# Two spectral-plus-MLP layers on one core: filter reversal in runs of four bins, merged mirror-class multiplies, rows of x issued from two queues

## The chip, the cores and the metric

The kernel runs on one core of one Trainium2 chip. The metric is the device time of one execution in microseconds (us). Most executions of a kernel here agree within 0.3%, which is some 3 us (the four of the kernel before lie within 2.7 us), and medians of four to six runs still leave about 1 us open; for smaller differences the document uses stage times from the profiles, one profiled execution of each kernel. In the profile of the kernel before, TensorE multiplies (6063 multiplies), VectorE and ScalarE work element by element and empty PSUM (775 and 504 instructions), POOL (GpSimd) and SP mostly issue DMA transfers (96 of POOL's 102 instructions).

## The reference, cut to what matters

```python
def _A_ref(x, w_r, w_i):                       # spectral layer
    X = rfft2(x.astype(float32)) * (w_r + 1j * w_i)
    return irfft2(X, s=(S, D)).astype(bfloat16)
def _B_ref(x, w1, b1, w2):                     # MLP
    h = x @ w1 + b1
    return (h * tanh(softplus(h))) @ w2

x = x + _A_ref(_layernorm(x), ...); x = x + _B_ref(_layernorm(x), ...)
x = x + _A_ref(_layernorm(x), ...); x = x + _B_ref(_layernorm(x), ...)
```

x is 2048 x 1024, the MLP is 3584 wide, everything is bf16 at the borders. Both layers of a kind share their weights.

## The kernel before

The Fourier transforms are factored into multiplies by constant tables. The first spectral layer goes: load x; row statistics on VectorE and ScalarE; a first transform (`s1`), which needs the rows of x in another order (XR) and tables scaled by each row's 1/deviation; then eight software-pipelined steps, each with the second transform (`s2`), the filter's preparation (`filter_bins`), the third transform and filter product (`s3`), and the way back (`i1`, `i2`); at last the back transform of the rows (`i4`).

Loading, and what runs beside it:

```python
    def prologue(self):
        for c in range(4):
            self.dma(sp, self.XS[:, 4*c:4*c+4, :], xt[...], f"x{c}", writes=...)
        # ... M0, IDF, JT from SP
        for q in range(4):
            for h in range(8):
                self.dma(sp, self.XR.ap[h:P:8, 32*q:32*q+32, :], xv[h][...], f"xr{q}", parts=[r])
        self.dma(sp, self.FD[:], self.con["FD"], "fd", writes=[self.r_fd])
        self.op(self.pool, lambda e: e.memset(self.EPS[:], 1e-5), writes=[self.r_eps, self.r_warm])
        self.warm(ACT.Sqrt)          # ScalarE: an activation that reads EPS, to load its table (1.28 us in the profile)
```

`first_scales` lets VectorE do the statistics of 10 tiles of x and ScalarE those of 6 (behind `warm` in ScalarE's queue), then one square root over all rows. The evacuations and the filter's reversal:

```python
    # s1: PSUM to Y
    if j % 2: ...activation...           # ScalarE
    else:     ...tensor_copy...          # VectorE
    # i2: PSUM to U; VectorE if the condition holds, else ScalarE
    if (g > 4 and (g < 7 or half == 0)) or (half == 0 and g % 2 and li): ...
    # filter_bins: a multiply by a reversed identity mirrors the bins, one multiply for each residue of 8
    for kd in (1, 2, 3):
        mov = wr.ap[:, c, src, :].rearrange("p (i k) -> p k i", k=8)[:, 7 - kd, :]     # every 8th bin
        fns.append(... e.matmul(ps[:, col:col + 64], jt[:, j:j + P], mov, ...))
```

## Time and profile before

| | before |
|---|---|
| median of the runs beside the changed kernel | 1054.78 us (1053.77 to 1056.46, 4 runs) |
| profiled span | 1051.8 us |
| first transform starts (first of its multiplies) | 25.25 us |
| eight steps start | 46.33 us |
| back transform of the first layer starts | 127.11 us |
| second layer: first transform, steps, back transform start | 550.72, 562.30, 633.67 us |

The three starts of the first layer are the rulers of this document. They are read off the timeline as the first multiply of each stage. "Steps" below means the time from the second start to the third, 80.78 us here; it contains the DMA round trip before the back transform, for which TensorE waits 11.95 us here, and which no part of the change touches.

### The profile page before, as it was taken

The numbers are of one execution on the slowest core, as the hardware profiler recorded it, in microseconds if no ns is written. First come the engines' busy times: TensorE is split into PE (matmuls) and PEld (weight loads), VectorE is DVE, ScalarE is ACT, GpSimd is POOL, SyncE is SP. The second block draws the span as 40 slices with busy tenths as digits, with TensorE's granted clock in tenths as the row PEclk, the third lists the DMA queues.
The fourth block names the chain that finished last, engine by engine and source line by source line (L and its number), as shares of the span: only waits on it lengthen the run. The fifth ranks groups of instructions, "written<-read, shape, count | busy, mean of one in ns | idle before, by whom it ended". The sixth has DMA issues, their size and how long they took to land. (4 is left out here: it accounts for less than half of the span.)

```text
span 1051.8 us, 14327 instructions
## 1 busy us (share of the span) xinstructions
PE 957.5 (91%) x6063; PEld 520.6 (49%) x6153; DVE 350.4 (33%) x775; ACT 339.0 (32%) x504; POOL 64.0 (6%) x102
## 2 busy tenths in 40 slices
PE   0699579999999999999969967899999999999998
PEld 0677465444444444444437746644444444444443
DVE  6887473340443100033327855526011100000111
ACT  6998264332000234400008844533300014331000
POOL 2042000000000000001521200000000000000000
PEclk9999789999999999999989986999999999999999
DMA  9778832455111121001941784144611112200000
GB/s 293 160 251 251 217 85 77 164 166 166 45 47 50 50 80 41 1 11 39 211 92 50 214 209 133 37 155 156 217 26 44 45 64 80 61 1 11 21 21 31
DMA packets 158480, 107.04 MB, mean 102 GB/s; under 512 B 80432, under 2 KB 138032, under 8 KB 158416
## 3 DMA queue, kind: packets, MB, share of 16 engines
q1 hardware_dynamic: 146272, 77.57, 25.7%
q0 software_dynamic: 9056, 26.87, 8.6%
q10 hardware_dynamic: 3088, 1.67, 0.6%
q8 instruction: 49, 0.80, 0.3%
q14 instruction: 15, 0.12, 0.1%
HBM read 80.85 MB, written 20.71 MB: 97 GB/s over the span
## 5 line engine op out<-in xcount | busy, mean ns | idle before, releaser
L963 PE MATMUL PS<-ARENA 128*128 128x512 bf16 (+1 forms) x1946 | 391.7, 361 | 10.3 <-DVE ARENA L938 7.2
L981 PE MATMUL PS<-ARENA 128*128 128x512 bf16 x1756 | 385.5, 379 | 1.9
L967 ACT ACTIVATE ARENA<-PS,B 128x512 bf16<-128x512 f32 (+1 forms) x248 | 159.8, 646 | 439.6 <-PE PS L963 439.6
L963 PEld LDWEIGHTS PS<-ARENA 128*128 128x128 bf16 x1984 | 194.6, 99 | 202.3 <-DVE ARENA L938 8.7
L981 PEld LDWEIGHTS PS<-ARENA 128*128 128x128 bf16 x1792 | 175.3, 98 | 211.4
L986 DVE TENSOR_TENSOR XS<-PS,XS 128x512 bf16<-128x512 f32 x64 | 44.3, 692 | 537.7 <-PE PS L981 537.7
L453 DVE BATCH_NORM_STATS2 BN<-XS 128x6 f32<-128x512 bf16 x104 | 67.2, 675 | 7.6 <-DMA XS<-in_A_x_dram 6.4
L902 DVE TENSOR_TENSOR XS<-PS,XS 128x512 bf16<-128x512 f32 (+1 forms) x40 | 29.1, 790 | 82.0 <-PE PS L888 82.0
L888 PE MATMUL PS<-MT,ARENA 128*128 128x32 bf16 (+1 forms) x768 | 24.6, 188 | 28.4 <-DMA ARENA<-u_scratch 23.9
L888 PEld LDWEIGHTS PS<-MT,ARENA 128*128 128x128 bf16 x768 | 23.2, 101 | 32.0 <-issue 26.3
L434 ACT ACTIVATE ARENA<-XS 128x1024 bf16<-128x1024 bf16 x24 | 25.3, 1055 | 36.6 <-DVE XS L902 31.5
L708 ACT ACTIVATE ARENA<-PS 128x1024 bf16<-128x1024 f32 x32 | 33.0, 1032 | 9.1 <-PE PS L704 9.1
L663 PE MATMUL PS<-FD,ARENA 128*128 128x256 bf16 (+1 forms) x312 | 32.5, 252 | 2.8 <-DVE ARENA L590 2.8
L737 ACT ACTIVATE ARENA<-PS 128x1024 bf16<-128x1024 f32 x32 | 33.0, 1030 | 4.2 <-PE PS L730 4.2
L730 PE MATMUL PS<-ARENA 128*128 128x256 bf16 x256 | 33.2, 273 | 0.6 <-DMA ARENA<-c_bt 0.5
L425 ACT ACTIVATE RS<-MV,EPS 128x1 f32<-128x1 f32 (+1 forms) x7 | 2.0, 292 | 98.5 <-DVE MV L456 96.2
L249 POOL DMA_DIRECT2D xn_scratch<-ARENA x15 | 8.5, 569 | 391.4 <-DVE ARENA L492 391.4
L712 DVE TENSOR_TENSOR ARENA<-ARENA 128x1024 bf16<-128x1024 bf16 x32 | 22.1, 690 | 27.5 <-ACT ARENA L708 22.2
L730 PEld LDWEIGHTS PS<-ARENA 128*128 128x128 bf16 x256 | 24.6, 98 | 10.5 <-PE PS L704 1.0
L663 PEld LDWEIGHTS PS<-FD,ARENA 128*128 128x128 bf16 x312 | 25.9, 98 | 7.2 <-DVE ARENA L590 3.2
L751 PE MATMUL PS<-ARENA,BD 128*128 128x256 bf16 x192 | 25.9, 273 | 0.4 <-DVE ARENA L777 0.2
L492 DVE TENSOR_SCALAR ARENA<-XS,MV,RS 128x1024 bf16<-128x1024 bf16 x48 | 25.3, 548 | 1.0
(69 smaller groups left out, 508.3 us busy)
## 6 DMA issues: line engine op xcount, KB each, us to landing
ARENA<-in_B_w_dram SPq DMA_DIRECT2D x56, 512.0 KB, 3.9
ARENA<-in_B_w_dram SPq DMA_DIRECT2D x56, 256.0 KB, 4.4
u_scratch<-ARENA SPq DMA_DIRECT2D x14, 512.0 KB, 3.6
ARENA<-u_scratch SPq DMA_DIRECT2D x14, 512.0 KB, 5.5
XS<-in_A_x_dram SPq DMA_DIRECT2D x4, 1024.0 KB, 8.8
ARENA<-in_A_x_dram SPq DMA_DIRECT2D x32, 128.0 KB, 3.2
w_scratch<-ARENA POOLq DMA_DIRECT2D x8, 512.0 KB, 4.8
ARENA<-w_scratch POOLq DMA_DIRECT2D x8, 512.0 KB, 5.3
```

The costliest lines, as they stand in the source:

```text
L453: self.op(self.dve, lambda e: e.bn_stats(self.BN[:, j, 6 * h:6 * h + 6], self.XS[:, j, 512 * h:512 * h + 512]), reads=[self.r_xs[j]], part ...
L663: fns.append(lambda e: e.matmul(dst, at(r), FD[:, t:t + dst.shape[-1] * 2], start=start, stop=stop))
L708: self.op(act, lambda e: e.activation(x.ap.rearrange("p a b -> p (a b)"), ps, ACT.Copy, scale=SIG), reads=banks, writes=[x.res])
L730: fns.append(lambda e, c=c, part=part: e.matmul(ps[:, c * 256:(c + 1) * 256], yk.ap[:, part, c * P:(c + 1) * P], t[:, (128, 0)[part]:(384, ...
L737: self.op(act, lambda e: e.activation(v.ap[:, :, i, :], src, ACT.Copy), reads=banks, parts=[v.res])
L751: fns.append(lambda e, dst=dst, part=part, c=c: e.matmul(dst, BD[:, c:c + P], mov(kd, part), start=(part == 0), stop=(part == 1)))
L888: fns.append(lambda e, l=l: e.matmul(ps[:, w * l:w * l + w], self.UT.ap[:, u0 + l, :], self.MT[:, 8 * lo:8 * lo + w], start=True, stop=True))
L902: self.op(self.dve, lambda e: e.tensor_tensor(xs, src, xs, ALU.add), reads=rb, parts=self.r_xs[lo:lo + nb])
L963: fns.append(lambda e, db=db, bank=bank, fl=fl: e.matmul(PS[:, bank, 0:w], wb.ap[:, db, fl * P:(fl + 1) * P], x.ap[:, db, tok], start=(db ...
L967: self.op(act, lambda e, bank=bank, ft=ft: e.activation(at.ap[:, ft, tok], PS[:, bank, 0:w], ACT.Mish, bias=self.B1[:, ft:ft + 1]), reads= ...
L981: fns.append(lambda e, i=i, ft=ft: e.matmul(PS[:, bank, :], at.ap[:, ft, t * P:(t + 1) * P], W2[ft].ap[:, h * 512:(h + 1) * 512], start=(i ...
L986: self.op(dve, lambda e: e.tensor_tensor(xs, PS[:, bank, :], xs, ALU.add), reads=[self.r_bank[bank]], writes=[self.r_xs[j]])
```

## The change

Its intent: have the rows of x in SBUF sooner by issuing them from two queues, ahead of the filter's loads; replace 12 small strided multiplies per filter group by 4 larger ones; merge the multiplies of the two mirrored classes in `s2`; and rebalance two kinds of evacuation.

```diff
@@ prologue
-                self.dma(sp, self.XR.ap[h:P:8, ...], xv[h][...], f"xr{q}", parts=[r])
+                prog = self.pool if q and h % 2 else sp
+                self.dma(prog, self.XR.ap[h:P:8, ...], xv[h][...], f"xr{q}{prog.name}",
+                         parts=[r], reads=[self.r_xs[15]] if prog is self.pool else [])
             self.r_xr.append(r)
-        self.dma(sp, self.FD[:], self.con["FD"], "fd", writes=[self.r_fd])
+            if q == 2:
+                self.dma(sp, self.FD[:], self.con["FD"], "fd", writes=[self.r_fd])
+        load_small("JT", 4 * P, BF)              # was ahead of XR
         self.op(self.pool, lambda e: e.memset(self.EPS[:], 1e-5), writes=[self.r_eps, self.r_warm])
@@ s1
-            if j % 2:
+            if j % 2 or li and j == 8:
@@ s2, second half: 4 multiplies of 256 columns and 8 of 128 become 8 of 256
-                            mm(dd, r + c, t + c * 256 + i * P, c == 0, c == 1)
+                            mm(dd[:, kd, :, :, :], r + c, t + c * 256, 256, c == 0, c == 1)
@@ i2
-            if (g > 4 and (g < 7 or half == 0)) or (half == 0 and g % 2 and li):
+            if (g > 4 and (g < 7 or half == 0)) or (half == 0 and g % 2):
@@ filter_bins
-                for kd in (1, 2, 3):
-                    mov = wr.ap[:, c, src, :].rearrange("p (i k) -> p k i", k=8)[:, 7 - kd, :]
-                    ... e.matmul(ps[:, col:col + 64], jt[:, j:j + P], mov, ...)
+                mov = wr.ap[:, c, src, :].rearrange("p (i k) -> p i k", k=8)[:, :, 4:8]
+                ... e.matmul(ps[:, col:col + 256].rearrange("p (i k) -> p i k", k=4), jt[:, j:j + P], mov, ...)
```

(The PSUM layouts of `s2` and of the filter's evacuation follow from these.)

More of the change, by code (lines that the diff above doesn't have):

```diff
@@ L378, in prologue, with load_small @@
         small = {}
-        for name, n, d in (("M0", P, BF), ("IDF", P, F32), ("JT", 4 * P, BF)):
+        def load_small(name, n, d):
             b = self.alloc(name, self.o[name], [n], d)
@@ L382, in prologue @@
             small[name] = b
+        load_small("M0", P, BF)
+        load_small("IDF", P, F32)
         self.M0, self.IDF = small["M0"], small["IDF"]
-        self.JT, self.r_jt = small["JT"].ap, small["JT"].res
         self.XR = self.alloc("XR", self.o["XR"], [P, P])
@@ L391, in prologue @@
             for h in range(8):
-                self.dma(sp, self.XR.ap[h:P:8, 32 * q:32 * q + 32, :], xv[h][:, 32 * q:32 * q + 32, :], f"xr{q}", parts=[r])
+                prog = self.pool if q and h % 2 else sp
+                self.dma(prog, self.XR.ap[h:P:8, 32 * q:32 * q + 32, :], xv[h][:, 32 * q:32 * q + 32, :], f"xr{q}{prog.name}",
+                         parts=[r], reads=[self.r_xs[15]] if prog is self.pool else [])
             self.r_xr.append(r)
-        self.dma(sp, self.FD[:], self.con["FD"], "fd", writes=[self.r_fd])
+            if q == 2:
+                self.dma(sp, self.FD[:], self.con["FD"], "fd", writes=[self.r_fd])
+        load_small("JT", 4 * P, BF)
+        self.JT, self.r_jt = small["JT"].ap, small["JT"].res
         self.op(self.pool, lambda e: e.memset(self.EPS[:], 1e-5), writes=[self.r_eps, self.r_warm])
@@ L660, in s2, with mm @@
             fns = []
-            def mm(dst, r, t, start, stop):
-                fns.append(lambda e: e.matmul(dst, at(r), FD[:, t:t + dst.shape[-1] * 2], start=start, stop=stop))
-            for i in range(2):
-                d = ps[:, i * 512:(i + 1) * 512].rearrange("p (r k) -> p r k", r=2)
-                if half == 0:
+            def mm(dst, r, t, n, start, stop):
+                fns.append(lambda e: e.matmul(dst, at(r), FD[:, t:t + n], start=start, stop=stop))
+            if half == 0:
+                for i in range(2):
+                    d = ps[:, i * 512:(i + 1) * 512].rearrange("p (r k) -> p r k", r=2)
                     for kd in range(2):
                         for c in range(2):
-                            mm(d[:, :, kd * P:(kd + 1) * P], 4 * kd + 2 * c + i, kd * 512 + c * 256, c == 0, c == 1)
-                    continue
-                for c in range(2):
-                    mm(d[:, :, 0:P], 8 + 4 * c + i, 1024 + c * 256, c == 0, c == 1)
+                            mm(d[:, :, kd * P:(kd + 1) * P], 4 * kd + 2 * c + i, kd * 512 + c * 256, 256, c == 0, c == 1)
+            else:
+                d3 = ps[:, 0:512].rearrange("p (s r k) -> p s r k", s=2, r=2)
+                for i in range(2):
+                    for c in range(2):
+                        mm(d3[:, i, :, :], 8 + 4 * c + i, 1024 + c * 256, 256, c == 0, c == 1)
+                dd = ps[:, 512:1024].rearrange("p (s r d k) -> p d s r k", s=2, r=2, d=2)
                 for kd in range(2):
-                    dd = d[:, :, P + kd * 64:P + kd * 64 + 64]
                     r, t = 10 + 4 * kd, (3 + kd) * 512
                     if g == 0:
-                        mm(dd, r + i, t, True, True)
+                        for i in range(2):
+                            mm(dd[:, kd, i, :, :], r + i, t, P, True, True)
                     else:
                         for c in range(2):
-                            mm(dd, r + c, t + c * 256 + i * P, c == 0, c == 1)
+                            mm(dd[:, kd, :, :, :], r + c, t + c * 256, 256, c == 0, c == 1)
             self.group(fns, reads=[self.Y.res, self.r_fd], writes=banks)
@@ L689, in s2 @@
             dst, src = zz[:, :, :, 256 * half:256 * half + 256], ps.rearrange("p (s r k) -> p s r k", s=2, r=2)
+            if half:
+                dst = dst.rearrange("p s r (b k) -> p s r b k", b=2)
+                src = ps.rearrange("p (b s r k) -> p s r b k", b=2, s=2, r=2)
             if half == 0 or g < 3:
@@ L853, in filter_bins @@
             for c in range(2):
-                for kd in (1, 2, 3):
-                    col = 512 * i + 192 * c + 64 * (kd - 1)
-                    mov = wr.ap[:, c, src, :].rearrange("p (i k) -> p k i", k=8)[:, 7 - kd, :]
-                    fns.append(lambda e, col=col, j=(j0 + c) * P, mov=mov: e.matmul(
-                        ps[:, col:col + 64], jt[:, j:j + P], mov, start=True, stop=True))
+                col = 512 * i + 256 * c
+                mov = wr.ap[:, c, src, :].rearrange("p (i k) -> p i k", k=8)[:, :, 4:8]
+                fns.append(lambda e, col=col, j=(j0 + c) * P, mov=mov: e.matmul(
+                    ps[:, col:col + 256].rearrange("p (i k) -> p i k", k=4), jt[:, j:j + P], mov, start=True, stop=True))
         self.group(fns, reads=[wr.res, r_jt], writes=banks)
@@ L869, in filter_bins @@
         for i in range(2):
-            src = ps[:, 512 * i:512 * i + 384].rearrange("p (c k i) -> p c k i", c=2, i=64)
+            src = ps[:, 512 * i:512 * i + 512].rearrange("p (c i k) -> p c k i", c=2, k=4)[:, :, 0:3, :]
             d3 = both[:, i, :, 0:384].rearrange("p c (k i) -> p c k i", i=P)
-            self.op(self.act, lambda e, d3=d3, src=src: e.activation(d3[:, :, :, 64:128], src, ACT.Copy),
+            self.op(self.act, lambda e, d3=d3, src=src: e.activation(d3[:, :, ::-1, 64:128], src, ACT.Copy),
                     reads=banks, parts=parts)
```

## The prediction

What the prediction infers of strided reads was measured later (e9: 64 columns 0.115 us strided, 0.029 contiguous; the changed kernel: a group of four 0.45 us). Its limit for rival (c), 7168 rows, is an estimate from one stop in the trace, 8.28 us after seven loads.

> **What bounds the kernel now.** The page's first part says TensorE, but that is an average over four stages: spectral layer, MLP, spectral layer, MLP.
>
> ```profile
> PE 957.5 (91%) x6063; PEld 520.6 (49%) x6153; DVE 350.4 (33%) x775; ACT 339.0 (32%) x504; POOL 64.0 (6%) x102
> L963 PE MATMUL PS<-ARENA 128*128 128x512 bf16 (+1 forms) x1946 | 391.7, 361 | 10.3 <-DVE ARENA L938 7.2
> L981 PE MATMUL PS<-ARENA 128*128 128x512 bf16 x1756 | 385.5, 379 | 1.9
> ```
>
> L963 and L981 are the MLP's two products, about 777 of the 1051.8 us. The diff touches neither. What it can move lies in the first 127 us (load, statistics, first spectral layer) and in 551 to 622 us (second spectral layer). So I read the timeline of the first 90 us next (columns: start, length, engine, line, operation, in brackets the idle time before it).
>
> ```profile
> 0.74 0.12 POOL L395 MEMSET EPS<- 128x32 f32 x1 [0.29 <-POOLq L1155]
> ...
> 2.04 0.20 ACT L418 ACTIVATE EPS<-EPS 128x1 f32<-128x1 f32 x1
> ...
> 6.37 1.06 ACT L434 ACTIVATE ARENA<-XS 128x1024 bf16<-128x1024 bf16 x1 [4.12 <-DMA XS<-in_A_x_dram]
> ...
> 7.04 32.19 SPq L249 DMA_DIRECT2D ARENA<-in_A_x_dram  x32
> ...
> 14.47 0.86 POOL L249 DMA_DIRECT2D ARENA<-in_A_w_r_dram  x1 [13.60 <-DMA XS<-in_A_x_dram]
> ...
> 22.30 0.31 ACT L425 ACTIVATE RS<-MV,EPS 128x16 f32<-128x16 f32 x1 [1.40 <-DVE MV L447]
> ...
> 24.12 3.34 DVE L567 TENSOR_SCALAR ARENA<-ARENA 128x128 bf16<-128x128 bf16 x20
> ...
> 31.11 3.59 PE L582 MATMUL PS<-ARENA 128*128 128x128 bf16 x32 [2.22 <-DMA ARENA<-in_A_x_dram]
> ```
>
> Three things are to be seen. The tiny memset of EPS is done at 0.86 us, ScalarE's first operation reads it, and behind that stand ScalarE's twelve statistics passes, which start when x's first quarter lands (6.37). POOL's first wait for the last quarter of x ends at 14.47. TensorE does wait for the re-laid-out rows of x (2.22 us at 31.11; twice more, 5.4 us together), which looks like the thing to remove.
>
> The windows view says whether that wait matters (columns: stretch, length, busy time and instructions of PE, PEld, DVE, ACT, POOL, clock, DMA share, GB/s).
>
> ```profile
> 25.00:45.00 20.00, 13.13 (x128) 11.55 (x128) 20.00 (x83) 19.86 (x54) 0.00 (x0) 1.00 0.92 208
> 46.30:69.10 22.80, 22.61 (x197) 18.59 (x200) 16.85 (x30) 20.08 (x26) 10.96 (x18) 1.00 0.59 186
> 69.10:103.50 34.40, 34.17 (x336) 27.62 (x338) 26.40 (x46) 30.51 (x37) 8.89 (x15) 1.00 0.85 268
> ```
>
> In 25 to 45 us (first transform) VectorE and ScalarE have no gap at all: scaling the tables and emptying PSUM is the bound there, and TensorE's waits for x are hidden. In 46.3 to 103.5 us (the software-pipelined steps with filter work) TensorE is 99% busy, with ScalarE close behind at about 88%. The waits view of 0 to 127 us shows how much slack ScalarE has:
>
> ```profile
> ACT ARENA L708 <- PE PS L704: 3.9, 6, 0.7
> ...
> ACT ARENA L872 <- PE PS L857: 2.2, 7, 0.4
> ```
>
> [...]on POOL the bias cast at 49.64 waits for its DMA, and the filter load queued behind starts only at 50.16. [...] The trace has SP at 32.19/32 = 1.0 us per issue, and a DMA share of 0.92 to 1.07 from 5 to 45 us: engines already full, little to win. [...]groups of 12 of 64 columns span 47.11 to 48.47 us, over 0.11 us apiece, while 32 multiplies of 32 columns at L888 take 1.03 us, 0.032 apiece. The difference is that L857 reads one bin in eight. I infer that the strided moving read costs it, per run and not per element; no run shows the latter yet.
>
> **The change part by part.**
>
> *Rows of x from two queues.* 12 of the 32 issues move from SP to POOL, and none may start before the last quarter of x is in. In the changed instruction order POOL now has these 12 copies before the EPS memset:
>
> ```
> L249 DMACopy ARENA<-in_A_x_dram 16x32x128 [waits x3]
> L249 DMACopy ARENA<-in_A_x_dram 16x32x128 x11
> L401 Memset EPS 128x32
> ```
>
> The memset, at 0.74 us before, therefore cannot run until 14.4 us plus twelve issues. Cost of an issue: POOL's filter loads (256 rows) take 0.72 us, its later loads from the scratch (1024 rows) 7.67/7 = 1.10. These have 512 rows, so between: about 0.83 us, twelve 10 us. The memset lands near 24.5, ScalarE's warm-up at 24.8, and only then can ScalarE do its first pass. VectorE stalls too, because after three tiles it combines ScalarE's sums. Following the two queues from ScalarE's start (passes of 1.18 us in pairs, VectorE 1.43 per tile, 0.42 per combination): tile 3 at +2.4, VectorE's tiles 4 and 5 to +5.6, combination of 6 and 7 to +7.5, tiles 8 to 10 to +11.8, then 12.2, 15.05, 15.5. So the square root comes 15.5 us after ScalarE's start: 24.8 + 15.5 = 40.3 against 22.30, **18.0 us later**, all on the path, since everything after needs it. The first transform still takes its 22.2 us: it was bound by VectorE and ScalarE and gains nothing from x being there.
>
> *Filter reversal.* 12 multiplies of 64 columns become 4 of 256 (192 used). At one column rate (L730: 8 of 256 columns span 0.87 us, 0.109 each) that is 0.44 instead of 1.31 us: 0.87 us per group, 7.0 us in eight groups. TensorE is the bound, but ScalarE follows. In the four steps from 46.3 to 69.1 us ScalarE has 20.9 us of effective work (19 evacuations at about 0.915 us, four L872 pairs at 0.87) after a start of 1.1 us, so only 0.8 of 22.8 us can go. In the next four, ScalarE needs about 29.1 us, or 27.3 with the two evacuations (g = 1, 3) now given to VectorE; TensorE 34.4 - 3.5 = 30.9 us. So 3.5 us go. Sum: **4.3 us**, call it 4.5. That stays below the 5.4 us or so of ScalarE waits in these steps (3.9 + 2.2, less one 0.67 in the drain). The strided PSUM read that L872 now makes should be free: L588 and L590 read PSUM with a stride of 128 elements, in 1.0 and 1.22 us per 1024, as others do contiguously.
>
> *Mirror classes merged.* 12 multiplies (4 of 256 columns, 8 of 128) become 8 of 256: 2048 columns before and after. L582 shows 8 of 128 columns in 0.45 us, 0.056 each, so they cost their columns: 4 x 0.109 + 8 x 0.055 = 0.87 against 8 x 0.109 = 0.87. Zero, in both spectral layers.
>
> *One evacuation of the second layer from VectorE to ScalarE.* From about 556 us VectorE had six back to back (7.04 us) and ScalarE six (6.12). Now five against seven at about 0.92: the other engine ends last. Zero, give or take 0.3.
>
> *JT and FD reordered*: both needed only after the first transform: zero.
>
> Sum: 1055.0 + 18.0 - 4.5 = **1068.5 us**.
>
> **The rivals.** (a) The delay of the memset is harmless and the filter saving shows alone: 1050 us. For it speaks only that the author meant to load earlier; against it, POOL's order and the wait on sem_POOL ahead of ScalarE's first activation. It would need POOL to run the memset ahead of waiting copies. (b) The wait for x was the bound and two queues remove 5.4 us: 1045 us with the filter. Against it: VectorE's gapless 20.00 of 20. (c) The issue on POOL is dearer because the DMA engines are full[...]: in the later scratch loads POOL stood 8.28 us after seven loads of 1024 rows. Here 12 x 512 = 6144 rows stay below those 7168, so I expect no such stop; with it, 1076. (d) Runs of four are read at the slow per-element rate: 4 x 256 columns at 1.7 ns is 1.74 us a group, 0.4 dearer than now, so no saving but a loss of up to 3 us: 1076 as well.
>
> **Range and chances.** The delay is 18 us with plus or minus 3 from POOL's issue time; the saving 4.5, between 2 and 7. Together 1062 to 1074, which I widen a little on both sides for the rivals: 1060 to 1075. The borders of 2% are 1033.9 and 1076.1. Faster than 1034 would need three times the filter's whole saving and no delay: 2%. Slower than 1076 needs (c) or (d) on top: 10%. Same: 88%.
>
> **What would show it.** In the changed kernel: the EPS memset at 23 to 27 us; ScalarE idle up to it; the square root at 38 to 43 us; the first transform again about 22 us long and without waits for x; the filter groups of four spanning about 0.44 us; step time in the steady part 7.7 instead of 8.6 us with ScalarE over 90%; the second spectral layer and both MLPs unchanged within 1 us. If the memset still runs before 1 us, the main step is wrong; if groups of four take 1 us or more, the filter step is; if the first transform gets shorter than 20 us, its bound was x after all.

## The result, and the profile after

The changed kernel takes 1066.69 us (median of 4 runs, 1065.89 to 1067.41) against 1054.78: **slower, by a ratio of 1.0111** (95% interval 1.0094 to 1.0129). Ratios here are the mean time of one kernel's runs over that of the other's timed beside it, so not quite the ratio of the quoted medians. The 1.1% lie inside the 2% borders that the prediction named.

The timeline of the changed kernel, at the places that the prediction showed of the one before:

```profile
0.75 1.28 ACT L424 ACT_TABLE_LOAD   x1 [0.75 <-PEq L1168]
...
6.14 25.70 SPq L249 DMA_DIRECT2D ARENA<-in_A_x_dram  x16
...
14.51 7.61 POOL L249 DMA_DIRECT2D ARENA<-in_A_x_dram  x12 [14.06 <-DMA XS<-in_A_x_dram]
22.11 0.14 POOL L401 MEMSET EPS<- 128x32 f32 x1
...
22.29 0.20 ACT L424 ACTIVATE EPS<-EPS 128x1 f32<-128x1 f32 x1 [20.26 <-POOL EPS L401]
22.40 1.04 ACT L440 ACTIVATE ARENA<-XS 128x1024 bf16<-128x1024 bf16 x1
...
24.74 0.28 DVE L451 TENSOR_SCALAR MV<-BN 128x2 f32<-128x2 f32 x1 [14.21 <-ACT ARENA L440]
...
38.03 0.31 ACT L431 ACTIVATE RS<-MV,EPS 128x16 f32<-128x16 f32 x1 [1.39 <-DVE MV L453]
```

The memset that ran at 0.74 us now runs at 22.11, behind twelve copies which wait for the last quarter of x. ScalarE stands idle for 20.26 us, VectorE for 14.21 us at its first use of ScalarE's sums, and the square root comes at 38.03 us instead of 22.30. One line that nobody thinks of as work, a memset of 32 columns, has come onto the path because it shares a queue with waits.

The windows view of the changed kernel (columns as in the prediction) for the first transform and for two stretches of the steps:

```profile
41.00:61.00 20.00, 15.20 (x128) 12.42 (x128) 20.00 (x82) 19.42 (x53) 0.25 (x1) 1.00 0.11 3
...
70.00:85.00 15.00, 14.54 (x118) 10.28 (x116) 14.36 (x27) 15.00 (x20) 7.26 (x13) 1.00 0.67 214
85.00:110.00 25.00, 24.16 (x225) 18.07 (x224) 22.39 (x37) 21.41 (x27) 8.27 (x14) 1.00 0.99 316
```

The first transform is bound by VectorE as before (20.00 of 20). All of x is there long before (DMA share 0.11), and it is not a bit shorter. In the early steps ScalarE is now the engine without a gap (15.00 of 15); later it is not.

| first layer, us | before | after | difference |
|---|---|---|---|
| first transform starts | 25.25 | 40.98 | +15.73 |
| its length, to the steps' start | 21.08 | 21.07 | 0.0 |
| steps, to the back transform's start | 80.78 | 77.95 | -2.83 |
| sum: back transform starts | 127.11 | 140.00 | +12.89 |

The profiled runs end 13.8 us apart, the medians 11.9: the profiled execution of the changed kernel was the slowest of its runs (1067.41 us), that of the kernel before faster than the four timed beside it (1053.58). About 1.3 us of the profiled pair comes at the hand-over to the second layer, where TensorE waits for a DMA (10.87 us against 9.54). That wait was 9.85 to 10.96 us in the ten other profiled runs, so I count it as scatter. From the start of the back transform to the end of the span the profiled executions take 923.9 to 926.0 us, whatever the kernel (e9 apart: 928.5); that much of a total's scatter lies outside the rulers.

### The profile page after: what moved, and what is told of

The parts are those of the page before. It is cut to its first block, busy times and chain, and to the rows that moved or that the text cites. A ratio compares the mean times of both kernels' runs of the same rounds, so it can differ in the third digit from the quotient of the medians.

```text
span 1065.6 us, 14183 instructions
## 1 busy us (share of the span) xinstructions
PE 959.8 (90%) x6033; PEld 513.0 (48%) x6033; DVE 352.0 (33%) x776; ACT 336.5 (32%) x503; POOL 71.0 (7%) x114
## 4 chain that ended last, share of the span: by engine, by line
PE 79%; DVE 9%; ACT 6%; DMA 3%; issue 1%; POOL 1%; SPq 0%; ACTq 0%; DVEq 0%
PE PS L976 36%; PE PS L994 36%; PE PS L669 2%; ACT ARENA L721 2%; DVE XS L915 1%; DVE ARENA L573 1%; DMA XS<-in_A_x_dram 1%; DVE ARENA L790 1%; DVE BN L459 1%; ACT ARENA L440 1%; DMA u_scratch<-ARENA 1%; DMA ARENA<-u_scratch 1%; DVE ARENA L951 1%; DVE ARENA L596 1%; PE PS L901 1%
## 5 line engine op out<-in xcount | busy, mean ns | idle before, releaser
L915 DVE TENSOR_TENSOR XS<-PS,XS 128x512 bf16<-128x512 f32 (+1 forms) x40 | 29.1, 790 | 82.1 <-PE PS L901 82.1
L721 ACT ACTIVATE ARENA<-PS 128x1024 bf16<-128x1024 f32 x32 | 33.8, 1058 | 8.5 <-PE PS L717 8.5
```

What stands on the lines that cost most here:

```text
L721: self.op(act, lambda e: e.activation(x.ap.rearrange("p a b -> p (a b)"), ps, ACT.Copy, scale=SIG), reads=banks, writes=[x.res])
L915: self.op(self.dve, lambda e: e.tensor_tensor(xs, src, xs, ALU.add), reads=rb, parts=self.r_xs[lo:lo + nb])
```

## The experiments

Each experiment was timed on one chip beside the kernel before, whose median there was 1055.61 us (e1 to e4), 1055.12 (e5 to e8) or 1054.85 (e9, e10). Medians of different groups are compared with that in mind. The stage times are from the profile of each.

| kernel | median us | ratio to before (95%) | steps start | steps | back transform starts |
|---|---|---|---|---|---|
| before | | 1 | 46.33 | 80.78 | 127.11 |
| changed | 1066.69 | 1.0111 (1.0094 to 1.0129) | 62.05 | 77.95 | 140.00 |
| e1 memset first | 1050.52 | 0.9958 (0.9946 to 0.9971) | 46.34 | 77.97 | 124.31 |
| e2 new loading only | 1070.98 | 1.0151 (1.0138 to 1.0164) | 61.96 | 82.26 | 144.22 |
| e3 filter reversal only | 1048.72 | 0.9939 (0.9927 to 0.9951) | 46.22 | 75.73 | 121.95 |
| e4 mirror classes only | 1054.23 | 0.9995 (0.9983 to 1.0007) | 46.27 | 80.64 | 126.91 |
| e5 changed, old loading | 1049.95 | 0.9951 (0.9937 to 0.9964) | 46.39 | 77.31 | 123.70 |
| e6 = e1, s1 half doubled | 1049.88 | 0.9952 (0.9939 to 0.9965) | 46.73 | 75.85 | 122.58 |
| e7 = e1, old evacuation in i2 | 1050.26 | 0.9962 (0.9947 to 0.9976) | 46.56 | 76.75 | 123.31 |
| e8 = e6 and e7 | 1048.81 | 0.9943 (0.9930 to 0.9955) | 46.62 | 74.56 | 121.18 |
| e9 contiguous read (wrong result) | 1049.01 | 0.9946 (0.9932 to 0.9959) | 46.76 | 74.27 | 121.03 |
| e10 = e3, s1 doubled | 1050.10 | 0.9954 (0.9941 to 0.9968) | 46.60 | 74.63 | 121.23 |

### e1: the memset first

```diff
+        self.op(self.pool, lambda e: e.memset(self.EPS[:], 1e-5), writes=[self.r_eps, self.r_warm])
         self.XR = self.alloc("XR", self.o["XR"], [P, P])
 ...
-        self.op(self.pool, lambda e: e.memset(self.EPS[:], 1e-5), writes=[self.r_eps, self.r_warm])
```

> The changed kernel with one line moved: the EPS memset ahead of the rows of x on POOL. Theory A (the late memset is the whole loss): memset before 1 us, square root near 22.3 us instead of 38.0, so 1066.7 - 15.7 = 1051 us, faster than the kernel before by about 4. Rival B (two queues crowd the DMA engines, so x itself and the statistics come late): 1060 or more even with the memset first. Side theory C (rows that come early leave TensorE without long bursts in the first transform, so it enters the steps at half rate): the first group of eight 256-column multiplies still takes about 1.9 us instead of 1.05.

POOL's timeline in this run:

```profile
0.74 0.12 POOL L387 MEMSET EPS<- 128x32 f32 x1 [0.29 <-POOLq L1168]
14.53 7.63 POOL L249 DMA_DIRECT2D ARENA<-in_A_x_dram  x12 [13.67 <-DMA XS<-in_A_x_dram]
```

The twelve copies wait and take as long as in the changed kernel; only the memset has moved, and the time is 1050.52 us as theory A said. The loss is the place of one instruction. Rival B falls: with the same two-queue traffic the steps start at 46.34 us, as before. The side theory's sign is there too: the first eight multiplies of the steps take 1.89 us, in the kernel before 1.05. "Half rate" and "full rate" are names for these two lengths of the same eight multiplies.

### e2: the new loading alone

The diff is the prologue hunk above, put into the kernel before.

> The kernel before with the new loading order alone (late memset included). Theory A: 1054.8 + 15.7 = 1070.5 us. With side theory C on top, 1 to 2 us more, 1072, and the first group of eight multiplies takes 1.9 us. Rival B: also slower, but then with the statistics waiting for x and not for the memset.

It takes 1070.98 us: the steps start 15.6 us later than before, and the steps themselves last 82.26 us, 1.5 longer than before although nothing in them was changed. Their first eight multiplies take 1.89 us here and 1.05 in the kernel before, the sign that theory C named. Whether it is the early rows that bring the half rate is another question: e3 and e5 bear on it.

### e3: the filter reversal alone

The diff is the `filter_bins` hunk, with its evacuation.

> The kernel before with the filter reversal alone. The prediction's sum says 4.3 us off: 1050.5 us, groups of four at 0.44 us. Rival D: the changed kernel gained only 3.0 us between the start and the end of the steps; if that is all the reversal gives, 1051.8 us. With theory C, TensorE enters at full rate here and the gain is over 3.

It takes 1048.72 us. That is the ratio 0.9939, or 6.4 us off, more than the predicted 4.3 and twice rival D's figure; the steps alone are 5.05 us shorter. The expectation missed on one point: TensorE did not enter at full rate here either, although the loading is that of the kernel before, which did. First the kernel before, then this run:

```profile
46.33 1.05 PE L663 MATMUL PS<-FD,ARENA 128*128 128x256 bf16 x8 [1.64 <-DVE ARENA L590]
```

```profile
46.22 1.89 PE L663 MATMUL PS<-FD,ARENA 128*128 128x256 bf16 x8 [1.19 <-DVE ARENA L590]
```

So with one queue the half rate may come or not.

### e4: the mirror classes alone

The diff is the `s2` hunk.

> The kernel before with the merged mirror classes alone. The prediction says zero, because the columns are the same: 1054.8 us within 0.7. Rival E: fewer weight loads (8 instead of 12) shorten 14 groups in two layers by 0.1 us or more each: 1053 us.

The ratio is 0.9995 with an interval that holds 1, and the steps are 0.14 us shorter. Zero, as predicted; rival E falls.

### e5: the changed kernel with the old loading

The diff undoes the prologue hunk in the changed kernel.

> The changed kernel with the old loading order (all rows of x from SP, memset first): filter reversal, merged mirror classes and the moved evacuations stay. Against the run with the memset first (1050.5) it shows what the second queue is worth once its trap is gone. Theory C (rows that come early leave TensorE at half rate on entry): this one is faster, about 1049.5. Rival G (early rows are worth something, up to the 5.4 us of waits for x): this one is slower, 1052 or more. It should stay above the filter reversal alone (1048.7) by 1.2, if theory F (the two evacuations moved to VectorE lengthen two steps by 0.6 us each) holds.

Its ratio is 0.9951 against e1's 0.9958, which the times cannot tell apart. What is clear is that the second queue gains nothing: the first transform lasts 21.08 us in both. The steps are 77.31 against 77.97 us, which speaks against rival G. It does not bear out theory C as stated, because TensorE enters at half rate here too, though the rows come late:

```profile
46.39 1.89 PE L663 MATMUL PS<-FD,ARENA 128*128 128x256 bf16 x8 [1.23 <-DVE ARENA L590]
```

Only the stretch at half rate is shorter: the next sixteen multiplies take 2.48 us, in e1 3.19, which is about the whole difference. So of the profiled kernels with one queue and no doubled multiplies, three enter at full rate (before, e4, e9) and two at half rate (e3, e5); the four with two queues (changed, e1, e2, e7) all enter at half rate. Early rows may make it likelier; that they cause it is not shown. Against e3 the steps are 1.58 us longer; theory F asked for 1.2, and the longer half-rate stretch can give the rest (the sixteen took 1.98 us in e3).

### e6: the first transform's second half twice over

```diff
+            if not li and j >= 8:
+                fns = fns + fns
             self.group(fns, reads=[self.r_xr[j // 4], ...], writes=banks)
```

(in e1)

> The memset first, and the multiplies of the first transform's second half issued twice over (same result; TensorE does needless work there). Theory C: TensorE is kept busy, reaches full rate before the steps begin, the first group of eight takes 1.05 us instead of 1.9, and the time falls by 1 to 1.5 us to 1049.3. Rival: the half rate on entry is hidden behind ScalarE, or the extra multiplies delay VectorE: 1050.5 or more.

The timeline of TensorE where the steps start, in the changed kernel:

```profile
62.05 1.89 PE L669 MATMUL PS<-FD,ARENA 128*128 128x256 bf16 x8 [1.19 <-DVE ARENA L596]
63.73 1.06 PE L870 MATMUL PS<-ARENA 128*128 128x256 bf16 x4
64.59 3.03 PE L669 MATMUL PS<-FD,ARENA 128*128 128x256 bf16 x16
```

and with the doubled multiplies (from e8, which enters like e6):

```profile
46.62 1.03 PE L671 MATMUL PS<-FD,ARENA 128*128 128x256 bf16 x8 [1.16 <-DVE ARENA L598]
47.49 0.62 PE L872 MATMUL PS<-ARENA 128*128 128x256 bf16 x4
47.95 1.69 PE L671 MATMUL PS<-FD,ARENA 128*128 128x256 bf16 x16
```

The same multiplies take nearly twice as long in the changed kernel, for some 5 us. Needless work beforehand cures it: the steps fall from 77.97 to 75.85 us, 2.1 us. The total fell by only 0.6 us in the median, and the intervals overlap, so the gain is shown for the stage and not for the whole time. What sets the rate, no run shows. In the kernel before, the waits for x gathered the first transform's multiplies into bursts of 32, 3.6 us long; when x is early they come, after the first 32, in twos of eight with gaps between (0.57 to 0.87 us in the changed kernel). Those three bursts ran at half rate themselves (0.11 us a multiply of 128 columns), and from 41.47 us on the multiplies took 0.056. Why the kernels with equal loading (before, e3, e5) entered differently (1.05, 1.89, 1.89 us) is not shown. What e6, e8 and e10 show is that extra work in the first transform is followed by a full-rate entry (1.03 us), three times out of three.

### e7: the two evacuations back to ScalarE

```diff
-            if (g > 4 and (g < 7 or half == 0)) or (half == 0 and g % 2):
+            if (g > 4 and (g < 7 or half == 0)) or (half == 0 and g % 2 and li):
```

(in e1)

> The memset first, and in the first layer the evacuations of g = 1 and 3 given back to ScalarE, as before. Theory F: the steps of 8.3 and 8.2 us become 7.65 like their neighbours, so 1.2 us less, 1049.3. Rival H (the prediction's view that ScalarE needs the relief): the time rises or stays at 1050.5.

In the changed kernel TensorE, and VectorE in front of it, look like this where g = 1 goes to VectorE (one fence per engine):

```profile
91.56 0.61 PE L764 MATMUL PS<-ARENA,BD 128*128 128x256 bf16 x4 [0.46 <-DVE ARENA L790]
```

```profile
90.29 1.22 DVE L790 CAST ARENA<-PS 128x1024 bf16<-128x1024 f32 x1
91.42 1.21 DVE L706 CAST ARENA<-PS 128x1024 bf16<-128x1024 f32 x1
```

TensorE waits for a PSUM bank that VectorE empties late, behind its filter products. The starts of the filter groups show what it costs: in e1 69.70, 78.02, 85.66, 93.89 us, so steps of 8.32, 7.64 and 8.23; in e7 69.90, 77.54, 85.19, 92.83, so 7.64, 7.65 and 7.64. The stage falls by 1.22 us, just as theory F said; the total moved by 0.3 in the median, within its scatter. In the stage the rebalancing was a loss, and rival H, which was also the prediction's own view, falls.

### e8: both

The diffs of e6 and e7 together, on e1.

> Both: memset first, old evacuations in the first layer, multiplies of the first transform's second half issued twice. If theories C and F are both right and independent: 1050.5 - 1.2 - 1.2 = 1048.1 us, as good as or better than the filter reversal alone (1048.7). If C is wrong: 1049.3.

The steps take 74.56 us: 1.29 less than e6 and 2.19 less than e7, so the two effects add. The total, 1048.81 us (1048.1 expected), beats the kernel before and the changed one and is as good as the filter reversal alone; these last two cannot be told apart.

### e9: the filter's multiplies read contiguous bins

```diff
-                    mov = wr.ap[:, c, src, :].rearrange("p (i k) -> p k i", k=8)[:, 7 - kd, :]
+                    mov = wr.ap[:, c, src, 64 * (7 - kd):64 * (7 - kd) + 64]
```

(in the kernel before; the result is wrong, relative error 0.049)

> Wrong results on purpose: the kernel before, where each of the 12 filter multiplies of 64 columns reads 64 neighbouring bins instead of every eighth one. Theory S (the strided read makes the 12 take 1.31 us): they fall to 0.4 to 0.7 us a group, as the 32 and 128 column multiplies elsewhere suggest, and the time falls like with the filter reversal, to about 1049. Rival (each multiply has a floor near 0.11 us, whatever it reads): 1.31 us a group and 1054.8 us as before.

TensorE's timeline in the kernel before, and then in this run:

```profile
47.21 1.55 PE L857 MATMUL PS<-ARENA 128*128 128x64 bf16 x12
48.59 1.72 PE L663 MATMUL PS<-FD,ARENA 128*128 128x256 bf16 x16
```

```profile
47.63 0.51 PE L857 MATMUL PS<-ARENA 128*128 128x64 bf16 x12
47.98 1.26 PE L663 MATMUL PS<-FD,ARENA 128*128 128x256 bf16 x12
```

Twelve multiplies now take 0.35 us (47.63 to 47.98), 0.029 apiece, where they took 1.38 (47.21 to 48.59), 0.115 apiece. Nothing but the stride of the read was changed, so the stride was the cost, and the floor of the rival falls. The time follows. 64 columns at a stride of eight cost 0.115 us, and 256 columns in runs of four (L872 in e8, four in 47.49 to 47.95) also 0.115. Why the stride costs that is not shown. No run here tries another stride.

### e10: the reversal alone, with the first transform doubled

The `filter_bins` hunk and the doubling of e6 from j = 4 on, in the kernel before.

> The kernel before with the filter reversal, one queue, old evacuations, and the multiplies of the first transform from j = 4 on issued twice. If half rate on entry is what the filter reversal alone still lost (its steps took 75.73 us, those of the doubled variant with two queues 74.56), the steps take about 74.6 us and the time is 1047.5. Rival: with rows of x that come late the doubled multiplies hold up VectorE, the first transform gets longer than 21.1 us and the time is 1049 or more.

The stage came out as expected, 74.63 us, with 0.2 us more in the first transform. The time did not: 1050.10 us (1048.35 to 1051.94) instead of 1047.5. So the rival's number came, but not by its cause: 0.2 us in the first transform cannot make up 2.6. The profiled execution is the fastest of the five (1048.35 us; its span is 1046.5). In it nothing takes the gain back: the back transform starts 0.72 us earlier than in e3, and the span ends 0.4 us earlier (1046.5 against 1046.9). Whether the full-rate entry is worth a microsecond of the total stays open.

## Why the prediction was right

The predicted 1068.5 us lies 1.8 above the measured 1066.69, inside the range. The main step held, the late memset. That the sum came out as close as this is partly luck: the delay was put 2.3 us too long and the saving 1.7 us too large, and that saving was itself a gain put too small, less two losses that were not foreseen.

- **The memset on the path: right, size 15.7 instead of 18.0 us.** Position, wait and consequence were as told, and e1 shows that this is the whole delay; rival (a), a harmless delay, falls with it. The memset itself came at 22.11 us, a little before the 23 to 27 that were named as the sign. The mis-sized term is POOL's time for an issue: 7.61/12 = 0.63 us, not 0.83. Interpolating by rows between two other kinds of transfer was wrong; these with 512 rows are cheaper than the filter's with 256 (0.72 us; 1.10 for 1024 rows), so the row count does not order them. The walk through the two statistics queues held: 15.6 us from ScalarE's start (22.40) to the square root (38.03), against 15.5.
- **The first transform gains nothing from early x: right.** 21.08 us before and 21.07 after, and in e1 and e5 alike. Rival (b), the tempting one, is refuted by this.
- **Filter reversal: right in kind, 6.1 instead of 4.3 us.** Groups of four take 0.45 us as worked out (67.35 to 67.80, first weight load to the next group's), and rival (d) is refuted. For the groups of twelve the prediction reckoned with 1.31 us, although the span it had read is 1.36. Compared at equal entry rate and with the old evacuations, e8's steps are 6.22 us shorter than before, 0.14 of it from the mirror classes; e10, the reversal alone, gives 6.15. Of this 2.4 us come in the first four steps, where the prediction allowed 0.8: it put ScalarE's floor there at 22.0 us (20.9 and 1.1), and e8 goes from the steps' start to the fifth filter group in 21.3, where before took 23.7. It had compared that floor with 22.8 us, to a slightly earlier point. In the later steps 7.65 instead of 8.59 us each was as predicted (7.7); in the changed kernel itself two of them took 8.2 to 8.3 (next point), and ScalarE was busy for 86% of 85 to 110 us, not the over 90% named as a sign. The evacuation that now reads PSUM with a stride takes 531 ns in the mean instead of 488, while ScalarE's contiguous ones beside it rose too (L708, now L721: 1026 to 1077), so little or nothing is due to the stride.
- **The evacuations given to VectorE: wrong sign.** The prediction counted them as relief (29.1 to 27.3 us of ScalarE's work). They cost 1.25 us (e1 to e7, e6 to e8). It had looked at ScalarE's total and not at VectorE's place in the chain of the same step.
- **Half rate on entry: not foreseen at all.** It costs 2.15 us in the steps (e1 to e6, e7 to e8), and 1.10 with one queue (e3 to e10).
- These three make up the -2.83 us of the steps: -6.22 + 1.25 + 2.15 = -2.82, against a predicted -4.5. The sum closes by construction, since e1, e6, e7 and e8 differ by just these two steps and e1's steps are as long as the changed kernel's (77.97 and 77.95); e10 is the independent check of its first term. The errors of 2.3 us in the delay and 1.7 in the saving leave 0.6 of the 1.6 us by which the predicted difference (13.5) exceeds the measured one (11.9); the other 1 us lies between the profiled pair and the medians, in the scatter.
- **Mirror classes, the moved evacuation of the second layer, FD and JT: zero, right.** e4 for the first; for the second, the first transform of the second layer takes 11.49 us (564.96 to 576.45) against 11.58.
- **Rival (c), a stop of POOL's issues: did not happen.** The twelve issues took 7.61 to 7.63 us, without a gap, in the changed kernel, e1 and e2. What stopped POOL for 8.28 us in the later scratch loads, the profile does not show.

## What to carry to other kernels

Before moving transfers to another engine's queue, read what stands behind them in that queue: here a memset of 0.14 us behind twelve waiting copies ran at 22.11 us instead of 0.74, and the diff does not show it, only the order of instructions does. A wait that a busy engine elsewhere hides is worth nothing when removed: here 5.4 us of waits for x went and the first transform stayed at 21.1 us. The same first multiplies of a stage may take 1.05 or 1.89 us; after the doubled multiplies they took 1.03. The profile's clock column does not tell the two apart: it reads 1.00 from 62 to 70 us of the changed kernel, where eight of them take 1.89 us. One has to look at the length of known multiplies. When moving work between two nearly full engines, compare the order within one step as well as the totals: the two evacuations given to VectorE cost 1.22 us of the steps (e1 to e7).
